# Attention and mixture of experts in one kernel: scores and foldings of a single batch over eight array tiles, and the second batch's exponentials by column on ScalarE

## The chip, the cores and the metric

One core of a Trainium2 chip runs the whole program. The metric is device time in microseconds, the median of several runs; lower is better. TensorE multiplies matrices into PSUM, VectorE, ScalarE and GpSimd work on tiles (GpSimd on SBUF alone), and SyncE issues nearly all DMA transfers.

## The reference

Eight batches, eight heads, 576 positions, head width 64. Each head first packs its keys and values with 32 learned queries `p`, and the positions then attend to the 32 packed rows. The result goes through four experts with a hidden width of 1024, weighted by given probabilities.

```
s = softmax(p k^T / 8);  packed = s v            # 32 rows a head
out = softmax(q packed^T / 8) packed             # 576 rows a head
x = out as (B*S, H*D);  pr = dp / (sum dp + 1e-9)
y = sum over e of pr[:, e] * (relu(x w1[e]) w2[e])
```

All data is fp32. Softmaxes subtract the row's maximum and divide by the sum plus 1e-9.

## The kernel before, in words

The attention's second product is never made for itself: the packed rows are multiplied into `w1` (`g_form`, the *folding*), and the experts' hidden layer comes from the attention weights times the folded matrix. Where fp32 accuracy is wanted from a single pass, an operand is split into a high part (a cast on ScalarE) and a low part (a subtraction); tiles `xh`, `xl` hold the two parts of a batch's attention weights, `ghl` those of a folded matrix, `st` and `tt` those of the second layer's operands. The second layer multiplies blocks by a seven-product scheme (`ORDER`).

**Units.** The main loop goes over 64 units: a batch and a chunk of 512 hidden columns (half of an expert). Batches go in pairs, chunks inside. The first units are batch 0 chunk 0, batch 0 chunk 1, batch 1 chunk 0, batch 1 chunk 1. In each unit there are seven products (`product`, 12 matmuls each), two products ahead their operands are made (`s_operand`: sums on VectorE, cast on ScalarE, subtraction on GpSimd), and in between come four projections of the next unit (`mm1_groups`, 12 matmuls each), foldings for a later chunk, and steps of the attention of later batches.

**Attention of a batch.** The eight heads are two groups of four (`g`). `pack_unit` loads K (L149) and V (L154, L157), makes scores (L122), takes the maximum (L171), exponentiates with the row sum (L177), turns the weights over (L192 to L195), multiplies them into V (L201), scales (L207 or L209) and puts the packed rows into `ppbd` (L105 or L104). `tok_unit` loads the queries (L230), makes scores, turns them by VectorE so that the 32 packed rows of each position lie along the free dimension (L237), takes maxima (L242), subtracts (L251), exponentiates all 576 columns at once (L254), sums (L257), divides (L263), turns back (L268) and splits into `xh` and `xl` (L269, L270 by L104 and L108). With `relief` scores are first copied out of PSUM by ScalarE (L169), the small scalings and additions run on ScalarE, and the exponential is 18 activations of 32 columns, each with its own maximum as bias (L247), in place of subtraction and one activation.

**Array tiles.** In scores and foldings a matmul has 64 rows and 32 columns: a quarter of the columns and half of the rows of the array. `cols(b, hh)` gives the half of a 64-column strip by head parity and batch parity, so that the two batches of a pair never use the same tile. For a pair the matmuls of both batches go out in turn, on eight tiles; for one batch four tiles are used, one group after the other. Each fp32 matmul is two instructions.

**The batches.** Batch 0 goes through an opening stage of some 40 us, with the chain of one group a step behind the other's, a warm-up of 22 matmuls with the identity and the forming of the first second-layer weights. Batch 1 (`second`) has a chain of generators: `wavefront` runs the pack units of its two groups in turn, then the two token units; `SECOND` says how many of its steps are emitted behind each product of units 0 and 1, and what is left is drained in unit 1 behind product 3, ahead of the folding of chunk 0. Later batches come as pairs, one group at a time; the third and fourth with `relief`. Batch 1 borrows tiles: K and queries lie in `xh2`, `xl2`, `xh3`, `xl3`, and V of its second group lies in `xl3`, which the second group's queries take over.

**Order.** Tile framework: the order on each engine comes from a planner that simulates the program and takes ready instructions by their place in the code; each engine runs its queue in order, and so does SyncE's DMA queue. By hand stand in order: `together` (the matmuls of a set stay together, and TensorE's other work keeps its side of it) and a few edges by `after`. PSUM is four double-bank tiles `dbl`.

Of the kernel before, what the change touches and what calls it, by code (L numbers as in the profile page):

```python
# [16 lines left out]
P = 128  # L17
# [22 lines left out]
def attention_moe(ctx: ExitStack, tc: tile.TileContext, q, k, v, p, dp, w1, w2, out):  # L40
# [56 lines left out]
    def cols(b, hh):  # L97

        i = (hh + b) % 2
        return slice(i * NPK, (i + 1) * NPK)  # L100
# [21 lines left out]
    def scores(bs, g, stationary, moving):  # L122

        pss = {b: dbl() for b in bs}
        calls = []
        for c in range(2):
            for j in range(2):
                for hh in range(2):
                    for b in bs:
                        p0 = 2 * j * NPK + cols(b, hh).start  # L130
                        calls.append(dict(
                            out=pss[b][p0:p0 + NPK, c, 0:HS], lhsT=stationary(b, 2 * g + j, hh),
                            rhs=moving[b][hh * D:(hh + 1) * D, j, c * HS:(c + 1) * HS], start=True, stop=True,
                        ))
        together(calls)
        return pss
# [3 lines left out]
    def pack_unit(bs, g, new, relief=False):  # L140
# [3 lines left out]
        for b in bs:  # L144
# [3 lines left out]
            kts[b] = new(b, [P, 2, S], "kt")  # L148
            nc.sync.dma_start(out=kts[b], in_=k[b][:, 2 * g:2 * g + 2, :])  # L149
        yield  # L150

        def load_v(b):
            vt, vr = new(b, [P, nfull, 4 * D], "vt"), new(b, [P, 4 * D], "vr")
# [6 lines left out]
        vt = load_v(bs[0])  # L160
        yield
        pss = scores(bs, g, lambda b, pr, hh: pts[b][hh * D:(hh + 1) * D, pr, :], kts)
        a1s, rss = {}, {}
        for b in bs:
            nb = small.tile([P, 1], F32, name="nb")
            a1s[b] = new(b, [P, S], "a1")
            a1v, raw = a1s[b].rearrange("p (c s) -> p c s", c=2), pss[b][:, :, 0:HS]
# [10 lines left out]
            rss[b] = small.tile([P, 1], F32, name="rs")  # L178
            if relief:
                nc.scalar.activation(out=rss[b], in_=sm, func=AF.Copy, bias=1e-9)  # L180
            else:
                nc.vector.tensor_scalar_add(rss[b], sm, 1e-9)
            nc.vector.reciprocal(out=rss[b], in_=rss[b])
        yield
        prs = slice(2 * g, 2 * g + 2)
        for b in bs:
            if b != bs[0]:
                vt = load_v(b)
            at = new(b, [P, len(SC), P], "at")
            ps = dbl()  # L190
            for c in range(nfull):
                tr(out=ps[:, 0, c * P:(c + 1) * P], in_=a1s[b][:, c * P:(c + 1) * P], identity=ident)  # L192
            tr(out=ps[0:r, 1, 0:P], in_=a1s[b][:, nfull * P:S], identity=ident)
# [4 lines left out]
            for c, (_, n) in enumerate(SC):  # L198
                for h in range(4):
                    p0 = h // 2 * 2 * NPK + cols(b, h % 2).start  # L200
# [13 lines left out]
            for hh in range(2):  # L214
                hi_of(
                    ppbd[b % 4][hh * D:(hh + 1) * D, prs, cols(b, hh)], psv[:, :, cols(b, hh)],
# [7 lines left out]
    def tok_unit(bs, g, new, eng=nc.vector, hi_eng=nc.scalar, lo_eng=nc.gpsimd, relief=False):  # L224
        qts, a2s = {}, {}
        for b in bs:
            if g == 0:
                xs[b] = (xpool.tile([P, NG, S], F32R, name=f"xh{b % 4}"), xpool.tile([P, NG, S], F32R, name=f"xl{b % 4}"))
            qts[b] = new(b, [P, 2, S], "kt")
            nc.sync.dma_start(out=qts[b], in_=q[b][:, 2 * g:2 * g + 2, :])  # L230
        yield
        pss = scores(bs, g, lambda b, pr, hh: ppbd[b % 4][hh * D:(hh + 1) * D, pr, cols(b, hh)], qts)
        for b in bs:
            a2s[b] = new(b, [P, S // 32, NPK], "a1")
            a2f = a2s[b].rearrange("p a n -> p (a n)")
            for c in range(2):
                nc.vector.transpose(out=a2f[:, c * HS:(c + 1) * HS], in_=pss[b][:, c, 0:HS])  # L237
        yield
        for b in bs:
            a2 = a2s[b]  # L240
# [442 lines left out]
```

## Time and profile before

| | us |
|---|---|
| median of 3 runs | 1300.62 (1300.3 to 1301.6) |
| the profiled execution, in all | 1302.57 |
| its span on the core | 1300.7 |
| TensorE busy | 1274.4 (98%) |
| VectorE busy | 954.7 (73%) |
| GpSimd busy | 859.4 (66%) |
| ScalarE busy | 495.7 (38%) |

The span is what the engines' records cover; the profiled execution's own time is longer by what lies before and behind. Busy time of TensorE is modelled from its pipelined matmuls. L67 is the helper of all plain matmuls, L70 of transposes and L75 of those in sets; L104 and L105 are `hi_of`, L108 is `lo_of`. So a row is read by its tiles, not by its line alone. Times in rows are counted from the start of the span.

### The profile page before, as it was taken

To read this page: it belongs to the slowest core of one execution; us is meant where nothing else is said; L and a number is where in the kernel's file an instruction comes from. 1 tells how busy PE (TensorE), PEld (TensorE's weight loads), DVE (VectorE), ACT (ScalarE), POOL (GpSimd) and SP (SyncE) were. 2 spreads that over 40 slices of the span, in tenths; PEclk is the share of its full clock that TensorE was granted. 3 is DMA by queue.
4 is the path that set the end of the run, shared out by engine and by line. 5 is a ranking of instruction groups with operands and counts; after the bars stand their busy time and mean duration, and the time that the engine had idled before them with its cause. 6 is when DMAs were issued, how large, how long until landed. Compare 5 with 4: busy or idle time off the path is not lost.

```text
span 1300.7 us, 26860 instructions
## 1 busy us (share of the span) xinstructions
PE 1274.4 (98%) x10764; PEld 1181.6 (91%) x10764; DVE 954.7 (73%) x1310; ACT 495.7 (38%) x886; POOL 859.4 (66%) x572
## 2 busy tenths in 40 slices
PE   6899999999999999999999999999999999999997
PEld 4789999998999989999999999999999999999997
DVE  6686677899975666987685666789668566666668
ACT  3444535646334333333335333333233433333321
POOL 4778888798995545666578454476558655555556
PEclk8999999999999999999999999999999999999998
DMA  9785646544465543454444456433345533434422
GB/s 350 282 305 204 218 165 226 181 149 167 148 219 194 173 155 124 164 176 155 144 154 164 150 174 194 160 115 115 130 156 203 164 130 123 124 110 153 130 98 73
DMA packets 89979, 218.42 MB, mean 168 GB/s; under 512 B 9088, under 2 KB 31744, under 8 KB 89856
## 3 DMA queue, kind: packets, MB, share of 16 engines
q1 hardware_dynamic: 89184, 216.57, 49.4%
q8 instruction: 86, 1.41, 0.4%
q14 instruction: 37, 0.30, 0.1%
q10 hardware_dynamic: 672, 0.15, 0.1%
HBM read 177.81 MB, written 38.87 MB: 167 GB/s over the span
## 4 chain that ended last, share of the span: by engine, by line
PE 84%; POOL 7%; DVE 5%; issue 2%; DMA 2%; ACT 1%; POOLq 0%; SPq 0%; DVEq 0%; ACTq 0%
PE dbl L67 77%; PE dbl L75 6%; POOL st L108 4%; POOL tt L108 2%; DVE sblk L361 1%; POOL b L398 1%; PE dbl L70 1%; POOL acc L478 1%; DVE ablk L336 1%; DMA xl<-in_q 1%; DVE nb L171 0%; DMA ablk<-in_w 0%; DVE ghl L108 0%; POOL xl L108 0%; DVE a L263 0%
## 5 line engine op out<-in xcount | busy, mean ns | idle before, releaser
L67 PEld LDWEIGHTS dbl<-st,tt 128*128 128x128 f32 x5376 | 730.3, 188 | 61.2 <-POOL st L108 36.2
L67 PE MATMUL dbl<-st,tt 128*128 128x288 f32 x5376 | 774.1, 298 | 5.1 <-POOL st L108 4.7
L108 POOL TENSOR_TENSOR st<-sblk,st 128x576 fp32r<-128x576 f32 x256 | 397.5, 1560 | 208.7 <-ACT st L104 203.5
L67 PE MATMUL dbl<-xh,ghl 128*128 128x288 f32 x2048 | 418.9, 296 | 5.4 <-DVE ghl L108 3.0
L108 POOL TENSOR_TENSOR st<-ablk,st 128x576 fp32r<-128x576 f32 x192 | 288.4, 1505 | 182.7 <-ACT st L104 175.1
L428 DVE TENSOR_TENSOR acc<-dbl,acc 128x576 f32<-128x576 f32 x385 | 289.1, 753 | 118.8 <-PE dbl L67 116.1
L67 PEld LDWEIGHTS dbl<-xh,ghl 128*128 128x128 f32 x2048 | 330.7, 189 | 7.9 <-DVE ghl L108 4.4
L336 DVE SCALAR_TENSOR_TENSOR ablk<-dbl,pbt 128x576 f32<-128x576 f32 x256 | 192.5, 753 | 163.6 <-PE dbl L67 162.3
L67 PE MATMUL dbl<-xl,ghl 128*128 128x288 f32 x1024 | 301.8, 295 | 0.7 <-DVE xl L108 0.7
L104 ACT CAST st<-sblk 128x576 fp32r<-128x576 f32 x256 | 173.0, 676 | 290.0 <-DVE sblk L361 198.4
L104 ACT CAST st<-ablk 128x576 fp32r<-128x576 f32 x192 | 129.7, 676 | 217.3 <-PE dbl L67 206.2
L67 PEld LDWEIGHTS dbl<-xl,ghl 128*128 128x128 f32 x1024 | 193.0, 189 | 0.9 <-DVE xl L108 0.9
L104 ACT CAST ghl<-dbl 128x512 fp32r<-128x512 f32 x128 | 74.8, 586 | 150.6 <-PE dbl L75 92.1
L361 DVE TENSOR_TENSOR sblk<-ablk 128x576 f32<-128x576 f32 x128 | 122.9, 961 | 9.5
L108 DVE TENSOR_TENSOR ghl<-dbl,ghl 128x512 fp32r<-128x512 f32 x128 | 87.4, 685 | 10.4 <-ACT ghl L104 6.7
L75 PE MATMUL dbl<-wraw,ppbd 64*32 64x512 f32 x1024 | 73.7, 600 | 0.2 <-DMA wraw<-in_w 0.2
L361 DVE TENSOR_TENSOR sblk<-ablk,sblk 128x576 f32<-128x576 f32 x64 | 66.3, 1036 | 5.8
L108 POOL TENSOR_TENSOR tt<-b,tt 128x512 fp32r<-128x512 f32 x42 | 62.2, 1491 | 2.1 <-ACT tt L104 2.0
L361 DVE TENSOR_TENSOR sblk<-sblk,ablk 128x576 f32<-128x576 f32 x64 | 57.9, 904 | 1.7
L478 POOL TENSOR_TENSOR acc<-acc,acc 128x576 f32<-128x576 f32 x28 | 47.4, 1702 | 16.2 <-DVE acc L428 16.1
L426 ACT COPY acc<-dbl 128x576 f32<-128x576 f32 x56 | 35.9, 641 | 41.2 <-PE dbl L67 40.6
L478 DVE TENSOR_TENSOR acc<-acc,acc 128x576 f32<-128x576 f32 x21 | 32.2, 1534 | 4.8 <-POOL acc L478 4.6
(90 smaller groups left out, 439.2 us busy)
## 6 DMA issues: line engine op xcount, KB each, us to landing
tt<-td SPq DMA_DIRECT2D x182, 512.0 KB, 4.3
wraw<-in_w SPq DMA_DIRECT2D x136, 256.0 KB, 3.1
td<-tt SPq DMA_DIRECT2D x56, 512.0 KB, 3.5
pbt<-pnd SPq DMA_DIRECT2D x32, 288.0 KB, 4.2
out<-acc SPq DMA_DIRECT2D x32, 288.0 KB, 2.3
kt<-in_k SPq DMA_DIRECT2D x14, 576.0 KB, 5.3
kt<-in_q SPq DMA_DIRECT2D x14, 576.0 KB, 5.4
vt<-in_v SPq DMA_DIRECT2D x15, 512.0 KB, 5.7
```

Source lines behind the costliest of these rows:

```text
L67: on_pe(nc.tensor.matmul(**kw))
L70: on_pe(nc.tensor.transpose(**kw))
L75: ins = nc.tensor.matmul(**kw).ins
L104: return nc.scalar.copy(out=dst, in_=src)
L108: return eng.tensor_tensor(out=dst, in0=src, in1=hi.bitcast(F32), op=ALU.subtract)
L336: nc.vector.scalar_tensor_tensor(out=a, in0=ps[:, :, 0:HS], scalar=0.0, in1=pbt[b][:, c * HS:(c + 1) * HS].rearrange("p (o t) -> p o t", o ...
L361: nc.vector.tensor_tensor(out=t, in0=blk(x), in1=blk(y), op=op)
L398: eng[m].tensor_tensor(out=blk[place], in0=blk[x], in1=blk[y], op=ALU.subtract)
L426: nc.scalar.copy(out=accs[b, i], in_=psv)
L428: nc.vector.tensor_tensor(out=accs[b, i], in0=psv, in1=accs[b, i], op=ALU.add)
L478: eng.tensor_tensor(out=m[dst], in0=m[x], in1=m[y], op=op)
```

## The change

`cols` takes the group too, so that the two groups of one batch use different tiles, as two batches do. `scores`, `pack_unit`, `tok_unit` and `g_form` take a list of items (batch, group) in place of a list of batches and one group.

- *Foldings of one batch* (four calls: opening stage, units 0, 1 and 2) put both groups' matmuls out in turn, eight tiles, into the two halves of one `dbl`. For a pair nothing changes.
- *Batch 1* has one pack unit and one token unit with both groups, in place of two interleaved ones each: K of both, V of both, scores of both side by side, then each group's rest in turn. Both run with `relief`. The chain has 9 + 12 steps instead of 12 + 10; `SECOND` stays.
- With `relief` the division of the token weights stays on the group's engine (VectorE for the first, GpSimd for the second), and the scaling of packed values is now always on VectorE (before, ScalarE with `relief`).
- Batch 0's opening stage keeps one unit for each group, and later pairs keep one group with two batches.

```diff
-    def cols(b, hh):
-        i = (hh + b) % 2
+    def cols(b, hh, g):
+        i = (hh + b + g) % 2
         return slice(i * NPK, (i + 1) * NPK)
...
-    def scores(bs, g, stationary, moving):
-        pss = {b: dbl() for b in bs}
+    def scores(items, stationary, moving):
+        pss = {it: dbl() for it in items}
...
-                    for b in bs:
-                        p0 = 2 * j * NPK + cols(b, hh).start
+                    for b, g in items:
+                        p0 = 2 * j * NPK + cols(b, hh, g).start
...
-        vt = load_v(bs[0])
+        both = items[0][0] == items[-1][0]
+        vts = {it: load_v(*it) for it in (items if both else items[:1])}
         yield
...
-            if relief:
-                nc.scalar.mul(ppn, ps[:, 0, 0:D], rss[b])
-            else:
-                nc.vector.tensor_scalar_mul(ppn, ps[:, 0, 0:D], rss[b])
+            nc.vector.tensor_scalar_mul(ppn, ps[:, 0, 0:D], rss[it])
...
-    def tok_unit(bs, g, new, eng=nc.vector, hi_eng=nc.scalar, lo_eng=nc.gpsimd, relief=False):
+    def tok_unit(items, new, engs=(nc.vector, nc.vector), hi_eng=nc.scalar, lo_eng=nc.gpsimd, relief=False):
...
     def g_form(bs, ch, raws):
-        for g in range(NG):
+        def run(items):
             ps = dbl()
-            pss = {b: ps[:, b % 2] for b in bs}
+            pss = {it: ps[:, i] for i, it in enumerate(items)}
             calls = []
             for hs in range(4):
-                pr, hh = 2 * g + hs // 2, hs % 2
-                rows = slice(hh * D, (hh + 1) * D)
-                for b in bs:
-                    c0 = (hs // 2) * 2 * NPK + cols(b, hh).start
+                for b, g in items:
+                    pr, hh = 2 * g + hs // 2, hs % 2
+                    rows = slice(hh * D, (hh + 1) * D)
+                    c0 = (hs // 2) * 2 * NPK + cols(b, hh, g).start
...
+        if len(bs) == 1:
+            run([(bs[0], g) for g in range(NG)])
+            yield
+        else:
+            for g in range(NG):
+                run([(b, g) for b in bs])
+                yield
...
+    ITEMS = [(1, g) for g in range(NG)]
     second = chain(
-        wavefront([pack_unit([1], g, second_tile(g)) for g in range(NG)], 1),
-        wavefront([tok_unit([1], g, second_tile(2 + g), nc.gpsimd if g else nc.vector) for g in range(NG)], 1),
+        pack_unit(ITEMS, second_tile(("xh2", "xl2")), relief=True),
+        tok_unit(ITEMS, second_tile(("xh3", "xl3")), (nc.vector, nc.gpsimd), relief=True),
     )
     SECOND = {0: (4, 3, 3, 3, 2, 2, 2), 1: (2, 20)}
```

## Rows read from the trace of the kernel before

**Rows 1.** The page, busy time of each engine: us, share of the span and instructions.

```profile
PE 1274.4 (98%) x10764; PEld 1181.6 (91%) x10764; DVE 954.7 (73%) x1310; ACT 495.7 (38%) x886; POOL 859.4 (66%) x572
```

**Rows 2.** The table by stretch: bounds and length in us, busy us and instructions of TensorE, its weight loads, VectorE, ScalarE and GpSimd, then the granted clock, the DMA share and GB/s. Four long stretches, and one of 4 us from a second table.

```profile
0.00:60.00 60.00, 46.44 (x478) 35.36 (x479) 37.55 (x68) 25.39 (x49) 34.60 (x30) 0.91 0.88 316
40.00:60.00 20.00, 17.74 (x213) 13.50 (x212) 12.58 (x21) 12.17 (x24) 15.15 (x11) 1.00 0.67 246
60.00:80.00 20.00, 19.84 (x164) 16.53 (x163) 18.87 (x32) 10.50 (x17) 18.66 (x13) 1.00 0.94 311
...
100.00:300.00 200.00, 197.84 (x1778) 182.85 (x1777) 154.29 (x199) 98.94 (x211) 172.16 (x116) 1.00 0.54 187
...
84.00:88.00 4.00, 4.00 (x32) 4.00 (x31) 1.57 (x3) 0.00 (x0) 1.12 (x1) 1.00 1.01 391
```

**Rows 3.** Waits of TensorE from 40 to 100 us, the two longest: what waited and for whom, us in total, times, longest.

```profile
PE dbl L70 <- ACT a L177: 1.0, 1, 1.0
PE dbl L67 <- ACT at L194: 0.8, 1, 0.8
```

**Rows 4.** Timeline of TensorE around the foldings (the matmuls from wraw and ppbd): start us, us, engine, line, operation, out<-in, shapes, count. Three of one batch, and one of a pair at 139.76; the row behind one shows what starts next.

```profile
41.34 1.92 PE L75 MATMUL dbl<-wraw,ppbd 64*32 64x512 f32 x16
...
77.05 1.92 PE L75 MATMUL dbl<-wraw,ppbd 64*32 64x512 f32 x16
78.91 1.86 PE L67 MATMUL dbl<-st,tt 128*128 128x288 f32 x12
...
90.25 1.92 PE L75 MATMUL dbl<-wraw,ppbd 64*32 64x512 f32 x16
...
139.76 1.09 PE L75 MATMUL dbl<-wraw,ppbd 64*32 64x512 f32 x16
140.78 1.86 PE L67 MATMUL dbl<-st,tt 128*128 128x288 f32 x12
```

**Rows 5.** Timeline of TensorE in the opening stage: the second half of the first folding, the first projection and the first product; the idle time before a row and what ended it stand at its end.

```profile
19.50 1.57 PE L75 MATMUL dbl<-wraw,ppbd 64*32 64x512 f32 x8 [0.19 <-DMA wraw<-in_w]
...
28.04 0.53 PE L67 MATMUL dbl<-xh,ghl 128*128 128x288 f32 x2 [1.86 <-ACT xh L104]
...
39.55 1.86 PE L67 MATMUL dbl<-st,tt 128*128 128x288 f32 x12 [1.17 <-POOL st L108]
```

**Rows 6.** Timeline of TensorE at the scores: of the second batch's pack unit (xh and xl hold its K), of its token unit (xh and xl hold its queries) with the product behind the first group's, and of a pair's pack unit with the product behind it.

```profile
47.58 1.18 PE L75 MATMUL dbl<-xh,pt 64*32 64x288 f32 x16
48.57 1.15 PE L75 MATMUL dbl<-xl,pt 64*32 64x288 f32 x16
...
63.06 1.17 PE L75 MATMUL dbl<-xh,ppbd 64*32 64x288 f32 x16
64.17 1.85 PE L67 MATMUL dbl<-st,tt 128*128 128x288 f32 x12
66.18 1.17 PE L75 MATMUL dbl<-xl,ppbd 64*32 64x288 f32 x16 [0.16 <-DMA xl<-in_q]
...
144.17 1.20 PE L75 MATMUL dbl<-kt,pt 64*32 64x288 f32 x32
145.30 1.87 PE L67 MATMUL dbl<-st,tt 128*128 128x288 f32 x12
```

**Rows 7.** Groups of instructions by line with each shape apart, whole run: line, engine, operation, out<-in, shapes, count, then busy us and mean ns of one, then idle time before. Exponentials by column (L247) and whole (L254), the subtraction on GpSimd, the copy of a pack's scores, the small copies of packed values on ScalarE, turns and maxima on VectorE.

```profile
L247 ACT ACTIVATE a<-a,m 128x32 f32<-128x32 f32 x72 | 16.3, 310 | 0.0
...
L237 DVE STREAM_TRANSPOSE a<-dbl 128x288 f32<-128x288 f32 x32 | 12.8, 453 | 3.3 <-PE dbl L75 3.3
...
L242 DVE TENSOR_REDUCE m<-a 128x18 f32<-128x576 f32 x16 | 11.7, 732 | 0.1
...
L254 ACT ACTIVATE a<-a 128x576 f32<-128x576 f32 x12 | 8.2, 686 | 15.7 <-DVE a L251 14.2 <-POOL a L251 1.4
...
L169 ACT COPY a<-dbl 128x576 f32<-128x576 f32 x4 | 2.4, 643 | 3.2 <-PE dbl L75 3.2
...
L104 ACT COPY ppbd<-dbl 64x64 f32<-64x64 f32 x8 | 1.6, 202 | 0.0
...
L251 POOL TENSOR_TENSOR a<-a,m 128x576 f32<-128x576 f32 x1 | 1.2, 1161 | 0.0
```

**Rows 8.** Timeline of ScalarE in a token unit of the third and fourth batch, in which the exponentials run by column: the first scaling of maxima, the first item's exponentials, and the second item's cast of turned weights.

```profile
245.57 0.22 ACT L245 ACTIVATE m<-m 128x18 f32<-128x18 f32 x1
...
246.36 3.93 ACT L247 ACTIVATE a<-a,m 128x32 f32<-128x32 f32 x18
...
268.40 0.68 ACT L104 CAST xh<-at 128x576 fp32r<-128x576 f32 x1 [1.81 <-DVE at L268]
```

**Rows 9.** Timelines around the second batch's token unit: SyncE's issue of the second group's queries, GpSimd's subtraction for the second group's low part, and TensorE's first projections from the batch's high parts (80.61) and from the second group's low part (86.99).

```profile
58.01 0.33 SPq L230 DMA_DIRECT2D xl<-in_q  x1
...
83.69 1.43 POOL L108 TENSOR_TENSOR xl<-at,xh 128x576 fp32r<-128x576 f32 x1 [1.60 <-ACT xh L104]
...
80.61 0.42 PE L67 MATMUL dbl<-xh,ghl 128*128 128x288 f32 x2
...
86.99 0.30 PE L67 MATMUL dbl<-xl,ghl 128*128 128x288 f32 x1
```

**Rows 10.** The table by stretch for TensorE alone: bounds, length, busy us and instructions, granted clock, DMA share, GB/s.

```profile
26.00:28.00 2.00, 0.17 (x2) 1.00 1.11 384
...
29.00:35.00 6.00, 5.75 (x24) 0.50 1.03 387
```

More of the change, by code (lines that the diff above doesn't have):

```diff
@@ L138, in attention_moe, with pack_unit @@
     pts = {}
-    def pack_unit(bs, g, new, relief=False):
+    def pack_unit(items, new, relief=False):
         nfull = S // P
@@ L177, in pack_unit @@
             nc.scalar.activation(out=a1v, in_=raw, func=AF.Exp, scale=SCALE, bias=nb, accum_out=sm)
-            rss[b] = small.tile([P, 1], F32, name="rs")
+            rss[it] = small.tile([P, 1], F32, name="rs")
             if relief:
-                nc.scalar.activation(out=rss[b], in_=sm, func=AF.Copy, bias=1e-9)
+                nc.scalar.activation(out=rss[it], in_=sm, func=AF.Copy, bias=1e-9)
             else:
-                nc.vector.tensor_scalar_add(rss[b], sm, 1e-9)
-            nc.vector.reciprocal(out=rss[b], in_=rss[b])
+                nc.vector.tensor_scalar_add(rss[it], sm, 1e-9)
+            nc.vector.reciprocal(out=rss[it], in_=rss[it])
         yield
[L185 to L189, printed above, removed]
+        for b, g in items:
+            it = b, g
+            if it not in vts:
+                vts[it] = load_v(*it)
+            vt = vts[it]
+            prs = slice(2 * g, 2 * g + 2)
+            at = new(b, g, [P, len(SC), P], "at")
             ps = dbl()
             for c in range(nfull):
-                tr(out=ps[:, 0, c * P:(c + 1) * P], in_=a1s[b][:, c * P:(c + 1) * P], identity=ident)
-            tr(out=ps[0:r, 1, 0:P], in_=a1s[b][:, nfull * P:S], identity=ident)
+                tr(out=ps[:, 0, c * P:(c + 1) * P], in_=a1s[it][:, c * P:(c + 1) * P], identity=ident)
+            tr(out=ps[0:r, 1, 0:P], in_=a1s[it][:, nfull * P:S], identity=ident)
             nc.scalar.copy(out=at[:, 0:nfull, :], in_=ps[:, 0].rearrange("p (c s) -> p c s", s=P))
@@ L199, in pack_unit @@
                 for h in range(4):
-                    p0 = h // 2 * 2 * NPK + cols(b, h % 2).start
+                    p0 = h // 2 * 2 * NPK + cols(b, h % 2, g).start
                     mm(
@@ L266, in tok_unit @@
             yield
-            a2t = new(b, [P, S], "at")
+            a2t = new(b, g, [P, S], "at")
             marks[b, g, "turn"] = nc.vector.transpose(out=a2t, in_=a2.rearrange("p a n -> p (a n)")).ins
@@ L502, in drain, with att_tile @@
             pass
-    def att_tile(b, shape, name):
+    def att_tile(b, g, shape, name):
         return att.tile(shape, F32, name=name, bufs=2 if name in ("kt", "a1") else 1)
@@ L563, in attention_moe, with second_tile, new @@
     AT_FIRST = ((4, pack_unit, 0), (7, pack_unit, 1), (9, tok_unit, 0), (12, tok_unit, 1))
-    def second_tile(n):
-        def new(b, shape, name):
-            if name == "kt" or name == "vt" and n == 1:
-                return xpool.tile(shape, F32, name=("xh2", "xl2", "xh3", "xl3")[n] if name == "kt" else "xl3")
-            return att_tile(b, shape, "kt" if name == "vr" else name)
+    def second_tile(names):
+        def new(b, g, shape, name):
+            if name == "kt" or name == "vt" and g == 1:
+                return xpool.tile(shape, F32, name=names[g] if name == "kt" else "xl3")
+            return att_tile(b, g, shape, "kt" if name == "vr" else name)
         return new
+    ITEMS = [(1, g) for g in range(NG)]
     second = chain(
-        wavefront([pack_unit([1], g, second_tile(g)) for g in range(NG)], 1),
-        wavefront([tok_unit([1], g, second_tile(2 + g), nc.gpsimd if g else nc.vector) for g in range(NG)], 1),
+        pack_unit(ITEMS, second_tile(("xh2", "xl2")), relief=True),
+        tok_unit(ITEMS, second_tile(("xh3", "xl3")), (nc.vector, nc.gpsimd), relief=True),
     )
@@ L590, in attention_moe @@
                     drain(back)
-                    back = make(pair, g, att_tile, relief=sb == 0)
+                    back = make([(n, g) for n in pair], att_tile, relief=sb == 0)
         gsteps = nothing
```

64 lines of the change are left out of this document (32 added, 32 removed).

## The prediction, made before the changed kernel ran

> **What bounds the kernel now.** I began with the page's busy shares: TensorE is busy 1274.4 of 1300.7 us, the other engines 38% to 73% [rows 1]. Next the table by stretch, to see where TensorE isn't full: it lacks 13.6 us in the first 60 us, 2.3 us of these in 40 to 60, then 0.2 us in 60 to 80 and 2.2 us in the 200 us after 100 [rows 2]. The reader is to see that from 60 us on the kernel is one long TensorE queue: a microsecond of matrix work taken out there is a microsecond off the end, if the operands still come in time. The same table names the neighbours: in 60 to 80 us VectorE has 18.87 and GpSimd 18.66 of 20 us, ScalarE 10.50. Third, TensorE's own waits in 40 to 100 us, where nearly all of the change lies: 1.0 us for an exponential (L177) and 0.8 us for the copy of turned scores (L194), most of the 2.3 us that are missing there [rows 3]. Last, TensorE's timeline for the price of each changed group, and the other engines' for the second batch's chain.
>
> The sum goes against the profiled execution's own time, 1302.57 us (span 1300.7 plus 1.87 around it). The median of the runs is 1300.62, that is 1.95 less; I carry the difference over to it.
>
> **The change part by part.**
>
> *Foldings of one batch.* Now both groups go one after the other, four array tiles each: 16 instructions from 77.05 until the next product starts at 78.91, 1.86 us. A pair's folding of one group has 16 instructions of the same shape in eight tiles: 139.76 to 140.78, 1.02 us [rows 4]. The changed folding of one batch has just this form, so each saves 0.84 us. Four calls: the one at 41.34 (unit 0), 77.05 (unit 1) and 90.25 (unit 2) lie in a full TensorE queue: 3 x 0.84 = 2.52 us. The fourth, in the opening stage, I cost at 0: its later matmuls wait for weights from DMA (its second half starts at 19.50), and what follows on the path, the first projection at 28.04, waits for ScalarE's cast of the turned weights, not for the folding [rows 5]. Side by side, the first half also waits for the weights of the second, inside that cover. If the cover were gone it could be worth -0.84 to +0.84 us; I leave it at 0.
>
> *Scores of the second batch.* Pack: 47.58 for the first group, 48.57 for the second, the last ends at 49.72 (48.57 + 1.15): 2.14 us. Tokens: 63.06 to 64.17, 1.11 us, and the second group's at 66.18, of the same length: 2.22 together. A pair's scores, 32 instructions, run 144.17 to 145.30, 1.13 us [rows 6]. Saved: 1.01 + 1.09 = 2.10 us. With the foldings 4.62 us of TensorE's queue go.
>
> *ScalarE's new work.* The exponentials of the tokens: 36 of 128x32 instead of two of 0.69 us. The 72 of the later batches took 16.3 us, 0.226 us each, so 36 cost 8.15 us, net +6.8 us [rows 7]. Score copies 2 x 0.64 = 1.3 us; the four small copies of packed values 4 x 0.20 = 0.8 us; some eight tiny scalings and additions, by the length of those copies about 1.6 us. Together near +10 us on ScalarE between about 43 and 80 us, where it has 22.7 of 40 us now: 33 of 40. It isn't full, but queued behind a run of six to eighteen exponentials (1.3 to 3.9 us) stand the casts of the products' operands, for which GpSimd and then TensorE wait. Two products of lookahead (1.7 us each, 78.91 to 80.61 [rows 4, 9]) with projections between them cover that. In the later relief stretch 18 exponentials ran as one block of 3.93 us [rows 8] without a wait of TensorE's there. I cost this delay at 0; without the cover one block would cost at most its 3.93 us.
>
> *What leaves VectorE and GpSimd.* One subtraction of 1.16 us on GpSimd, one on VectorE, the four small copies [rows 7] and the tiny ones: about 3 us of VectorE where it is the fullest. As TensorE isn't waiting for it, I count 0 for itself; it shortens the chain below. Scaling of the packed values in the next two batches goes back to VectorE: four small operations, hidden, 0 (bounds: -1.0 us, the longest of TensorE's waits in rows 3, and +0.8 us, four of the small copies).
>
> *The pack chain, moved.* It has 4 + 3 + 3 steps in unit 0 as before, but the scores come in product 0's share instead of product 1's, up to 43.2 - 0.84 = 42.4 instead of 47.6. Each group's chain gains the copy (0.64 us) ahead of the maximum. Projections and products that stood before the scores now can stand between scores and transposes. The two waits of 1.0 and 0.8 us there may go, or grow by the two copies: bounds -1.8 to +1.3 us; I take 0. On SP the second batch's V loads and the token loads move up together; the second group's queries go into the tile in which its V lay, so they wait for the pack's last use of it: issued at 58.01, they let the scores start at 66.18 with a wait of 0.16 us [rows 6, 9]. Now both groups' token scores wait for that load; nothing on TensorE but they depends on it, and products are at hand to go first.
>
> *The token chain.* Before: scores of the first group at 63.06, second group's low part done at 83.69 + 1.43 = 85.12, used by TensorE at 86.99 (the first use of either part of this batch is at 80.61) [rows 6, 9]. That use moves up by what is saved ahead of it, 0.84 + 1.01 + 1.09 + 0.84 = 3.8 us, to 83.2. The new chain starts when the second group's queries are there, now for both groups: 66.2 less the 3 to 6 us by which the pack moves up, 60 to 63. By the old latency of the second group, 85.12 - 66.18 = 18.9 us, it ends at 79 to 82, in time. By the later relief stretch it takes 2.4 us (four turns of 0.45, one maximum of 0.73, less one that overlaps with the first scaling), 22.8 us from the first scaling (245.57) to the second item's cast (268.40) [rows 7, 8], and 2.1 us for cast and subtraction, 27 us in all: it ends at 87 to 90, 4 to 7 us late. In that stretch nobody waited for it and ScalarE also cast formed weights; and after 80 us, where ScalarE and VectorE now mostly wait (84 to 88 us: 0 and 1.57 of 4 us [rows 2]), there is room for the chain's end. TensorE can also put remaining products first, as it did. I lie nearer to the old latency: 61.5 + 18.9 + half of the exponentials' net 6.8 us is 83.8, some 0.6 us late; I take 1.0 us of wait, with 0 and 7 as ends.
>
> *The Trainium skill on this.* After the token scores TensorE's next instruction is a product (64.17), while VectorE takes 0.9 us per group to empty the banks: nothing waits for that [rows 6, 7]. The Trainium skill, "TensorEngine Tiling (Array Packing)", section Performance Considerations (PSUM Bottleneck), says that tiling makes TensorE faster but not the emptying of PSUM, which can then become the bound. By that rule the scores' 2.10 us would buy nothing; the case is the third rival below, and the row at 64.17 speaks against it.
>
> Sum: -2.52 - 2.10 + 1.0 = -3.6 us: 1302.57 - 3.6 = 1298.97 in the profiled execution, 1300.62 - 3.6 = 1297.0 as a median.
>
> **Rivals.**
> 1. *The second batch is late by as much as was saved.* The chain takes 23 to 25 us from 61.5 and the wait is 2 to 4 us and more, without other loss: at 4 us -4.62 + 4 = -0.6, 1300.0 (1298.0 to 1303). For it: rows 8's latency, and 36 exponentials in one in-order queue. Against: the earlier start and the emptier engines after 80 us.
> 2. *Slower: the same wait, and the clock falls.* In the opening TensorE was busy 0.17 of 2 us in 26 to 28 us, and the granted clock stood at 0.50 for 29 to 35 us [rows 10]: six to seven us at 1.2 instead of 2.4 GHz, some 3.3 us lost. If the second batch's operands come so late that TensorE stands still for about 5 us near 80 us, the clock goes too: -4.62 + 5 + 3.3 = +3.7, 1304.3. The clock went in the opening after a wait of 1.86 us [rows 5]; with its 3.3 us the result is slower than before from a wait of 1.3 us, and by more than a measurement's doubt from 3.9, that is, where the low part is done at 87.1 or later: scores at 61 and a chain of 26 us. For it: the queries' load that holds both groups. Against: TensorE has two products and half of the projections to put into such a hole, and these would keep its clock up.
> 3. *Narrow tiles buy nothing in the scores* because emptying four half banks takes 1.8 us against 1.13 of matrix work: -2.52 + 1.0 = -1.5, 1299.1. Against it: the pair's scores at 144.17 are followed by a product without a gap [rows 6]. The rule is that of the Trainium skill, "TensorEngine Tiling (Array Packing)", PSUM Bottleneck, cited above.
> 4. *More than the sum:* the waits of 1.8 us go too and none comes: -4.62 - 1.8 = -6.4, 1294.2.
>
> **How the numbers follow.** Forecast, 1295.3 to 1298.5: 0.48. Rival 1: 0.22. Rival 2: 0.14. Rival 3: 0.06. Rival 4: 0.10. A measurement tells 0.2% from nothing, 2.6 us: faster is under 1298.0, slower over 1303.2. Faster: of the forecast 0.43, rival 4 0.10, together 0.53. Slower: rival 2's 0.14 and 0.02 of rival 1: 0.16. Within: 0.31. Range: from 1293.8 (most of rival 4) to 1303.2 (rivals 1 and 3 but for a rest, not rival 2).
>
> **What would show it.** Right: foldings of one batch with 16 instructions to the next in about 1.0 us and scores with 32 in 1.13 at four and two places, TensorE's instruction count the same, and TensorE's waits in 40 to 95 us at 1 to 3 us. The second batch's first projection at about 77, not 80.6 us. Wrong: a TensorE wait for the second batch's high or low part, or for an operand of a product behind a block of exponentials; a granted clock under 1 after 40 us; a wait for the queries' load of over 1 us; the first product starting at another time than 39.55 us [rows 5]. The forecast falls if this chain costs over 2 us, or if the planner's order later in the kernel shifts by as much.

## The result, and the profile after

The changed kernel takes 1311.94 us (median of 6 runs, 1309.66 to 1313.32) against 1300.67 us for the kernel before in the same sitting: ratio 1.0081, 95% interval 1.0071 to 1.0091. It is slower, by 0.8%; the forecast was 1297.0 us, and the range ended at 1303.2. The profiled execution took 1311.35 us, its span 1309.3 us. One run of an experiment below, *token exponential whole*, was disturbed (1375.87 us): it is left out of that kernel's median, and as it is the traced one, no trace of that kernel is read.

The busy times on the page of the changed kernel, beside [rows 1]:

```profile
PE 1273.8 (97%) x10764; PEld 1181.9 (90%) x10764; DVE 950.7 (73%) x1303; ACT 505.0 (39%) x930; POOL 856.1 (65%) x571
```

TensorE's count is the same and its busy time hardly is less, though matrix work was saved. ScalarE gained 9.3 us. What was saved came back as matmuls at a lower clock, as the rows below show, and the longer span is idle time: 35.5 us of TensorE's span instead of 26.3. Where it lies, TensorE's timeline of the changed kernel shows (start us, us, operation, count; idle time before a row at its end). The line numbers have moved: L178 is the exponential of the pack unit (L177 before), L247 the exponentials by column.

```profile
39.50 1.86 PE L67 MATMUL dbl<-st,tt 128*128 128x288 f32 x12 [0.54 <-POOL st L108]
41.29 1.09 PE L75 MATMUL dbl<-wraw,ppbd 64*32 64x512 f32 x16
42.17 0.40 PE L75 MATMUL dbl<-xl,pt 64*32 64x288 f32 x1
...
48.62 1.33 PE L70 MATMUL dbl<-ident,a 128*128 128x128 f32 x5 [5.28 <-ACT a L178]
49.61 3.23 PE L67 MATMUL dbl<-st,tt 128*128 128x288 f32 x12
...
62.98 0.67 PE L75 MATMUL dbl<-xh,ppbd 64*32 64x288 f32 x2
64.08 0.40 PE L75 MATMUL dbl<-xl,ppbd 64*32 64x288 f32 x1 [0.44 <-DMA xl<-in_q]
...
65.21 1.85 PE L67 MATMUL dbl<-st,tt 128*128 128x288 f32 x12
...
79.72 4.98 PE L67 MATMUL dbl<-st,tt 128*128 128x288 f32 x24 [3.08 <-POOL st L108]
84.63 1.09 PE L75 MATMUL dbl<-wraw,ppbd 64*32 64x512 f32 x16
85.65 1.85 PE L67 MATMUL dbl<-st,tt 128*128 128x288 f32 x12
...
99.46 3.45 PE L67 MATMUL dbl<-st,tt 128*128 128x288 f32 x24
...
118.28 1.95 PE L75 MATMUL dbl<-wraw,ppbd 64*32 64x512 f32 x32
```

Three rows of the kernel before to hold against these: the product behind the turns, the first products of unit 2, and the first folding for a pair.

```profile
51.26 1.82 PE L67 MATMUL dbl<-st,tt 128*128 128x288 f32 x12
...
92.11 3.60 PE L67 MATMUL dbl<-st,tt 128*128 128x288 f32 x24
...
109.97 1.95 PE L75 MATMUL dbl<-wraw,ppbd 64*32 64x512 f32 x32
```

The first product starts where it did (39.50; 39.55 in [rows 5]). The folding with 32 instructions, the first for a pair, starts at 118.28; in the kernel before it starts at 109.97. This stretch, from the first product to that folding, is 78.78 us long against 70.42: 8.36 of the 8.6 us of span. I call it *the stretch* and use it for the experiments too, since it begins behind the opening stage.

TensorE's waits in the changed kernel, 40 to 100 us (us in total, times, longest), against the two of [rows 3]:

```profile
PE dbl L70 <- ACT a L178: 5.3, 1, 5.3
PE dbl L67 <- POOL st L108: 3.1, 1, 3.1
PE dbl L67 <- POOL xl L108: 0.9, 1, 0.9
PE dbl L70 <- DVE ppn L209: 0.8, 2, 0.4
```

The tables by stretch, with all engines first (to be held against [rows 2]) and then TensorE alone with its granted clock:

```profile
40.00:60.00 20.00, 13.91 (x190) 11.69 (x189) 10.32 (x16) 13.48 (x31) 12.11 (x9) 0.83 0.69 257
60.00:80.00 20.00, 16.48 (x141) 14.98 (x141) 13.81 (x20) 15.06 (x54) 10.00 (x8) 1.00 0.64 238
```

```profile
46.00:48.00 2.00, 0.00 (x0) 0.58 1.01 377
48.00:50.00 2.00, 1.38 (x7) 0.50 0.31 106
...
80.00:82.00 2.00, 2.00 (x12) 0.61 0.13 49
```

In the first long wait, and behind the second, the granted clock fell from 1.00 to about 0.50, that is from 2.4 to 1.2 GHz. The product at 49.61 took 3.23 us, [rows 4] has 1.86 for twelve matmuls; the 24 matmuls at 79.72 took 4.98 us, two such products at full clock, at 68.50 and at 73.28, took 3.36.

The account from the first product of unit 0 to that of unit 2 (99.46; 92.11 in the kernel before), where the kernel lost 59.96 - 52.56 = 7.40 us:

| | us |
|---|---|
| foldings: 3 x 0.84 | -2.52 |
| pack scores: 42.17 to 43.35 instead of 2.14 us | -0.96 |
| token scores: 62.98 to 65.21, 2.23 us with the wait for the queries inside; before 2.22 and a wait of 0.16 | -0.15 |
| waits: 5.28 + 3.08 + 0.94 + 2 x 0.41, before 1.02 + 0.76 + 0.33 | +8.01 |
| clock: 3.23 - 1.82, 4.98 - 3.36, turns 0.99 - 0.52 | +3.50 |
| sum | +7.88 |

The sum is 0.48 us more than was lost; which small rows hold that is not traced.

**Where the first wait comes from.** ScalarE in the changed kernel, 43 to 50 us:

```profile
45.46 0.59 ACT L104 CAST ghl<-dbl 128x512 fp32r<-128x512 f32 x1 [0.76 <-DVE ghl L108]
45.95 1.19 ACT L170 COPY a<-dbl 128x576 f32<-128x576 f32 x2
...
47.70 0.78 ACT L178 ACTIVATE a<-a,nb 128x576 f32<-128x576 f32 x1
```

Scores end at 43.35. ScalarE copies them out only at 45.95, behind its casts for the products and the folding, of which the last is shown; then come maximum, scaling and exponential, and only then the turns at 48.62. In the kernel before, product 1 and a projection stood ahead of the scores (47.58), not between scores and turns. By then VectorE was through with the folding's low parts and waited for the scores, so that the turns followed after 1.02 us. VectorE's first maximum in the kernel before:

```profile
48.82 0.76 DVE L171 TENSOR_REDUCE nb<-dbl 128x1 f32<-128x576 f32 x1 [0.38 <-PE dbl L75]
```

Now the scores come while ScalarE is still busy with casts, the turns are the very next thing in TensorE's queue, and product 1 stands behind them.

**Where the second comes from.** ScalarE again, 68 to 79 us, and the GpSimd row that follows from it:

```profile
68.59 4.13 ACT L247 ACTIVATE a<-a,m 128x32 f32<-128x32 f32 x19
...
73.15 1.39 ACT L247 ACTIVATE a<-a,m 128x32 f32<-128x32 f32 x6
...
74.95 1.39 ACT L247 ACTIVATE a<-a,m 128x32 f32<-128x32 f32 x6
...
76.34 1.17 ACT L247 ACTIVATE a<-a,m 128x32 f32<-128x32 f32 x5
77.40 1.24 ACT L104 CAST st<-sblk 128x576 fp32r<-128x576 f32 x2
```

```profile
78.15 2.91 POOL L108 TENSOR_TENSOR st<-sblk,st 128x576 fp32r<-128x576 f32 x2 [8.33 <-ACT st L104]
...
90.39 1.44 POOL L108 TENSOR_TENSOR xl<-at,xh 128x576 fp32r<-128x576 f32 x1 [0.21 <-ACT xh L104]
```

36 exponentials (19 + 6 + 6 + 5) run from 68.59 to 77.5; between the blocks stand two copies of results and a small addition, but no cast of a product's operand. GpSimd, which makes the low parts, stands still for 8.33 us; TensorE lives on its lookahead and then waits 3.08 us. The row at 90.39 is the second group's low part, the end of the token chain.

### The profile page after: what moved, and what is told of

Read it like the earlier page. It is cut to its first block, busy times and chain, and to the rows that moved or that the text cites. A ratio compares the mean times of both kernels' runs of the same rounds, so it can differ in the third digit from the quotient of the medians.

```text
span 1309.3 us, 26888 instructions
## 1 busy us (share of the span) xinstructions
PE 1273.8 (97%) x10764; PEld 1181.9 (90%) x10764; DVE 950.7 (73%) x1303; ACT 505.0 (39%) x930; POOL 856.1 (65%) x571
## 4 chain that ended last, share of the span: by engine, by line
PE 83%; DVE 7%; POOL 6%; ACT 2%; issue 1%; DMA 1%; DVEq 0%; SPq 0%; ACTq 0%; POOLq 0%
PE dbl L67 77%; PE dbl L75 5%; POOL st L108 3%; DVE sblk L368 2%; POOL tt L108 1%; DVE ablk L343 1%; PE dbl L70 1%; DVE acc L450 1%; ACT a L247 1%; DVE a L263 0%; DVE ghl L108 0%; POOL xl L108 0%; DVE acc L435 0%; DVE nb L172 0%; POOL acc L485 0%
```

## Experiments: the two long waits

Theory: the loss comes from these two places, and the eight tiles are innocent. Rivals: VectorE's load, the scalings moved to it, or the tiles themselves. Medians, ratios to the kernel before in the same sitting (1300.7 to 1301.4 us), and the stretch in the profiled execution:

| kernel | median us | ratio, 95% interval | stretch us |
|---|---|---|---|
| before | 1300.67 | | 70.42 |
| the change | 1311.94 | 1.0081 [1.0071, 1.0091] | 78.78 |
| turns behind product 1 | 1310.35 | 1.0067 [1.0052, 1.0082] | 77.24 |
| token exponential whole | 1309.81 | 1.0053 [1.0032, 1.0074] | |
| both of these | 1304.92 | 1.0028 [1.0019, 1.0038] | 73.35 |
| steps spread over three units | 1305.37 | 1.0035 [1.0024, 1.0047] | 74.06 |
| no `relief` for batch 1 | 1308.12 | 1.0050 [1.0035, 1.0065] | 75.66 |
| scalings on ScalarE | 1311.17 | 1.0073 [1.0058, 1.0088] | 78.53 |
| TensorE kept busy in the hole | 1311.83 | 1.0078 [1.0061, 1.0094] | 84.03 |
| foldings alone | 1302.16 | 1.0008 [0.9998, 1.0018] | 70.14 |
| scores and late foldings, steps in turn | 1302.67 | 1.0012 [1.0003, 1.0021] | 71.92 |
| foldings, batch 0's by group | 1302.56 | 1.0002 [0.9993, 1.0011] | 72.14 |
| scores and all foldings, steps in turn | 1302.72 | 1.0010 [1.0001, 1.0018] | 72.72 |
| before, turns later | 1301.81 | 1.0015 [1.0006, 1.0024] | 71.25 |
| foldings by group, turns later | 1305.16 | 1.0027 [1.0018, 1.0037] | 70.82 |
| in turn, turns later | 1304.62 | 1.0029 [1.0018, 1.0040] | 72.59 |

Each stretch is that of one execution. In eight of these traces the first product starts at 37.3 to 38.1 us, in the other seven, the kernel before and the change among them, at 39.5 to 40.3. In the kernel before the granted clock stood at 0.50 from 29 to 35 us [rows 10]; in *foldings alone*, whose first product starts at 37.71, it was 1.00 on the mean of the opening. In four of the early ones unit 0's folding then waits 0.30 to 0.91 us for weights from DMA, in none of the late ones. So an early start can come back in part as a longer stretch, and a microsecond of difference between an early and a late trace says nothing.

**Turns behind product 1.** Of the chain's steps, product 0 issues three instead of four, so the first group's turns come behind product 1.

```diff
-    SECOND = {0: (4, 3, 3, 3, 2, 2, 2), 1: (2, 20)}
+    SECOND = {0: (3, 4, 3, 3, 2, 2, 2), 1: (2, 20)}
```

> The changed kernel with SECOND[0] starting 3, 4 in place of 4, 3: the first group's turns are emitted behind product 1 instead of behind product 0, nothing else. Theory: TensorE's wait of 5.3 us at 48.6 us and the half clock from 49 to 53 us go, the wait at 79.7 us stays: 7 us off the changed kernel, about 1304.5. Rival (the chain is what takes the time, wherever its turns are queued; it ends later and the wait near 80 us grows by as much): 1309 to 1312.

TensorE's timeline of this kernel:

```profile
47.72 0.77 PE L70 MATMUL dbl<-ident,a 128*128 128x128 f32 x5 [0.90 <-ACT a L178]
...
60.38 0.40 PE L75 MATMUL dbl<-xl,ppbd 64*32 64x288 f32 x1 [1.66 <-DMA xl<-in_q]
...
76.03 4.81 PE L67 MATMUL dbl<-st,tt 128*128 128x288 f32 x24 [3.08 <-POOL st L108]
```

The time is the rival's. The first wait is gone, 0.90 instead of 5.28 us, but the stretch is only 1.54 us shorter: the token scores now wait 1.66 us for queries, three waits of 0.5 to 0.75 us stand in the rest of the pack chain, and the second long wait stays whole.

**Token exponential whole.** `relief` off in the token unit alone.

> The changed kernel with relief off in the second batch's token unit alone (one exponential of 576 columns, subtraction on VectorE or GpSimd); pack unit as changed. Theory (36 exponentials ahead of the products' casts make the wait at 79.7 us): that wait, its clock loss and the 0.9 us at 88.8 go, 5 to 6 us off the changed kernel, near 1306. Rival (VectorE, relieved by it, becomes what is waited for, as in the run without relief, where a folding's low part came 2.1 us late): 1308 to 1310.

The three runs took 1304.93, 1309.81 and 1310.02 us, so this gain is known only roughly, some 2 us; the median is the rival's.

**Both of these.**

```diff
-        tok_unit(ITEMS, second_tile(("xh3", "xl3")), (nc.vector, nc.gpsimd), relief=True),
+        tok_unit(ITEMS, second_tile(("xh3", "xl3")), (nc.vector, nc.gpsimd)),
...
-    SECOND = {0: (4, 3, 3, 3, 2, 2, 2), 1: (2, 20)}
+    SECOND = {0: (3, 4, 3, 3, 2, 2, 2), 1: (2, 20)}
```

> Both repairs: turns behind product 1 (SECOND[0] = 3, 4, 3, ...), and the token unit without relief; pack unit with relief, scores and foldings in eight tiles. Theory (two separate waits): both gone, 1304 to 1306, that is 4 to 6 us off the run with the turns later alone, still above the kernel before by the waits for the queries and for packed values. Rival (VectorE late): 1308 or more.

Alone they gave 1.6 and some 2 us, both together 7.0: while one long wait stands, most of what the other gives back is waited out further on. Theory's 1304 to 1306 us for both together came true. **Spread** is the other way to take both waits away: the turns behind product 1, and the token unit with `relief` as in the change, but its steps dealt out so that a few exponentials at a time lie between the casts.

```diff
-    SECOND = {0: (4, 3, 3, 3, 2, 2, 2), 1: (2, 20)}
+    SECOND = {0: (3, 4, 3, 1, 1, 1, 1), 1: (2, 2, 2, 20)}
```

> The changed kernel with SECOND = {0: (3, 4, 3, 1, 1, 1, 1), 1: (2, 2, 2, 20)}: the turns behind product 1 as in the run before, and the token unit's steps spread over two more products, so that two casts of products' operands stand ahead of most of the second group's exponentials on ScalarE. Theory: beside the first wait the second one (3.1 us, and about 1.5 us of clock) goes too, 4 us off the run with the turns later alone, near 1306. Rival (the second batch is then late at its own projections by as much): 1309 to 1312.

It gains 6.6 us with all 36 exponentials by column, 5.0 us more than the turns behind product 1 alone, and no wait of TensorE in the stretch is longer than 1.0 us. So the second wait came from their lying in one block, not from their cost.

**The rivals.** Without `relief` in both units, and with the next batches' small scalings back on ScalarE:

> The changed kernel with relief off in both units of the second batch: no score copies, one exponential for 576 columns, small steps on VectorE. Theory (two waits: turns queued ahead of product 1, and products behind 36 exponentials): the wait at 79.7 us (3.1), the one at 88.8 (0.9) and the clock's loss behind them (about 1.7) go, the wait at 48.6 us shrinks from 5.3 to about 4 and its clock loss of about 2 us stays: near 1304.5 us. Rival one (ScalarE's new work is the whole cause): below 1299. Rival two (one unit for both groups is the whole cause): 1310 or more.

> The changed kernel with the packed values of the third and fourth batch scaled on ScalarE again, nothing else. Theory: the wait of TensorE for L209 between 240 and 300 us (1.5 us) goes, about 1310.4. Rival (that wait is only another one's shadow): 1311.9, the same.

Without `relief` the first wait is still 4.13 us: the copies of scores were a small part of it, and now the maxima wait on VectorE (45.35) behind the low parts of the folding. The 1308.12 us lie between the theory's 1304.5 and rival two's 1310: a wait of 2.08 us for a folding's low part, which VectorE makes, is new at 84.45. The scalings' place takes TensorE's wait for them from 1.5 to 0.4 us and moves its busy time between 240 and 300 us from 58.24 to 59.33 (59.75 in the kernel before, whose work lies some 8 us earlier), but the time only within its interval: not shown to cost anything in the end.

**The clock alone.** 22 matmuls with the identity fill the hole behind the pack scores; their result isn't used.

> The changed kernel with 22 matmuls of the identity with itself (as in the warm-up) between the second batch's pack scores and its turns, into the hole of 5.3 us; nothing waits for them. Theory (the hole also costs the clock): granted clock 1.00 from 44 to 54 us, product 1 in 1.8 instead of 3.2 us, about 2 us off, 1310. Rival (what the clock lost there is waited for later anyway): 1311.9, the same.

Product 1 took 1.83 us at a granted clock of 1.00, but the time is that of the change, as the rival said. TensorE's timeline further on, in an execution that was the slowest of the four (1317.11 us; the others 1310.58 to 1313.01):

```profile
64.66 0.66 PE L76 MATMUL dbl<-xl,ppbd 64*32 64x288 f32 x1 [2.65 <-DMA xl<-in_q]
66.76 3.25 PE L68 MATMUL dbl<-st,tt 128*128 128x288 f32 x12
```

What the clock gave back, the scores waited out for the queries in this execution, and the clock fell there instead (0.50 from 64 to 70 us).

## Experiments: what the saved matrix work is worth

The kernel without either long wait was still 3.7 us slower than before; in its trace the token scores wait 2.00 us for queries, the packed values 1.2 us for VectorE, and unit 0's folding 0.91 us for weights. So the savings themselves were tried.

**Foldings alone** (all four; batch 1's chain as before).

> Only the foldings of a single batch go over eight tiles (columns by group too); the second batch keeps its interleaved units, narrow scores and whole exponentials, and packed values of the third and fourth batch are scaled on ScalarE as before. Theory (the loss sits in the second batch's chain, the foldings save what their rows say): 3 x 0.84 us off the kernel before, about 1298.1 us against its 1300.7. Rival (eight tiles give nothing back in a single batch, or the loss comes with the new columns): 1300.7 or more.

TensorE's timeline of this kernel at unit 0's folding and the turns:

```profile
39.49 1.04 PE L75 MATMUL dbl<-wraw,ppbd 64*32 64x512 f32 x2
40.83 1.74 PE L75 MATMUL dbl<-wraw,ppbd 64*32 64x512 f32 x14 [0.30 <-DMA wraw<-in_w]
42.50 1.87 PE L67 MATMUL dbl<-st,tt 128*128 128x288 f32 x12
...
49.39 0.77 PE L70 MATMUL dbl<-ident,a 128*128 128x128 f32 x5 [1.94 <-ACT a L178]
```

With the groups' matmuls alternating the folding needs all four weight tiles at its start. Here it starts 1.8 us sooner than in the kernel before, the tiles are not there, and it took 3.01 us instead of 1.86. In the trace of the change, with a late first product, the same folding found its weights there (41.29 to 42.17). The next three leave the alternating out, or test it:

```diff
-        if len(bs) == 1:
+        if bs == [1]:
             run([(bs[0], g) for g in range(NG)])
```

In the first and the second, batch 0's foldings go group by group. Their tiles still differ by the group, so the second group's matmuls run beside the first's: at unit 0 the trace has 16 instructions in 1.09 us, the row of an eight-tile folding. The narrow folding of the expectations was therefore never run; what these kernels change at unit 0 is that the second half's weights are needed later. *In turn* also means that the wide scores are kept, `relief` is off for batch 1, and the two groups' steps alternate as in the kernel before, with `SECOND[0] = (2, 2, 3, 3, 0, 2, 2)`.

> Second batch's scores of both groups on eight tiles, and wide foldings in units 1 and 2 only; the rest as before: the two groups' steps interleaved stage by stage, scores behind product 1, the exponential as one activation, no copies of scores, batch 0's foldings with four tiles. My theory: the change lost by the place of the turns in TensorE's queue and by the block of exponentials ahead of the casts, not by the eight tiles. Then both long waits (5.3 and 3.1 us) are gone, the clock stays at 1.00 from 40 to 100 us, and the matrix work saved counts: 2.1 us of scores and 1.7 us of foldings, less up to 1 us because both groups' scores wait for the second group's queries: 1297.5 to 1298.5. Rival: what is saved comes back as small waits for GpSimd, VectorE and the queries' load, since these engines are nearly full from 60 to 80 us: 1300 to 1302, ratio 0.999 to 1.001. A third, that eight tiles of one batch in themselves do harm, would give 1303 or more.

> Only the second batch's foldings (units 1 and 2) on eight tiles, all else as before. My theory: the kernel with all foldings wide gained nothing because unit 0's folding waits for four weight tiles at once and pushes the pack chain back; without it the two others are worth what they save, 2 x 0.84 us = 1.7: 1299.5. Rival: the products behind them wait for GpSimd's operands as much longer as the folding is shorter: 1301.2, the time before.

> As the kernel in turn, but with the foldings of the opening and of unit 0 on eight tiles as well. My theory: unit 0's folding loses by waiting for four weight tiles what it saves in matrix work: the same as the kernel in turn, or up to 1 us more. Rival: it gives its 0.84 us: about 1 us less than the kernel in turn.

None of these four gains as a median; the theories of a gain, 1298.1 us, 1297.5 to 1298.5 and 1299.5, failed. In the foldings by group much of that is the clock: its four runs at a mean granted clock of 0.998 or 0.999 took 1299.82 to 1300.35 us, its seven at 0.994 and 0.995 took 1301.65 to 1304.21; the five of the kernel before at 0.998 in that sitting took 1300.31 to 1301.33. So where the clock held, the medians of these few runs differ by 0.3 of the 2.5 us: the eight tiles do no harm in the foldings, and little good. The traced execution is the slowest, 1304.21 us. TensorE's timeline of it shows both, the saving that is waited out and the fall of the clock:

```profile
41.41 1.09 PE L75 MATMUL dbl<-wraw,ppbd 64*32 64x512 f32 x16
...
50.83 0.95 PE L70 MATMUL dbl<-ident,a 128*128 128x128 f32 x5 [1.94 <-ACT a L178]
51.43 3.23 PE L67 MATMUL dbl<-st,tt 128*128 128x288 f32 x12
...
80.56 1.83 PE L67 MATMUL dbl<-st,tt 128*128 128x288 f32 x12 [0.98 <-DVE s L264]
...
95.63 1.86 PE L67 MATMUL dbl<-st,tt 128*128 128x288 f32 x12 [0.69 <-POOL st L108]
```

VectorE behind that folding, first in the kernel before, then in this one:

```profile
43.43 1.80 DVE L361 TENSOR_TENSOR sblk<-ablk,sblk 128x576 f32<-128x576 f32 x1
45.18 1.29 DVE L108 TENSOR_TENSOR ghl<-dbl,ghl 128x512 fp32r<-128x512 f32 x2
```

```profile
43.52 1.81 DVE L371 TENSOR_TENSOR sblk<-ablk,sblk 128x576 f32<-128x576 f32 x1
45.27 1.29 DVE L108 TENSOR_TENSOR ghl<-dbl,ghl 128x512 fp32r<-128x512 f32 x2
```

Both executions start the first product within 0.1 us of each other (39.55 and 39.63). TensorE finishes the folding some 0.8 us sooner, VectorE takes it up at the same time as before, 45.2, since it is busy with sums for the products. The turns stand at 50.83 against 50.74 [rows 3 has their wait, 1.0 us; here 1.94]. At unit 0 nothing is saved, and behind the longer wait the clock fell to 0.50 in this execution: 3.23 us for the product behind the turns, product 2. Behind the other two foldings 0.98 and 0.69 us are waited out for operands, against 0.84 us that each saves.

**Is it the turns or the feeders?** The last three put one more product between scores and turns, in the kernel before and in two variants. Counted from 0, as in the rest of this text, it is product 2; the expectations call it product 1.

```diff
-    SECOND = {0: (4, 3, 3, 3, 2, 2, 2), 1: (2, 20)}
+    SECOND = {0: (4, 2, 3, 4, 2, 2, 2), 1: (2, 20)}
```

> The kernel before with one move: product 1 ahead of the turns of the second batch's pack unit, the second group's packed values behind product 2. It takes out a wait of 1.0 us for the exponential and one of 0.8 us for the copy of turned scores, and no matrix work. If TensorE's queue is the bound: 1301.3 less 1.0 to 1.8 us, 1299.5 to 1300.3. If VectorE, ScalarE and GpSimd set the pace, product 1's early end is waited out further on: 1301.3, as before.

> All three foldings of a single batch behind the opening on eight tiles (batch 0's by taking its two groups one behind the other on different tiles), and the same move of the turns. Theory A (the wait for the turns and the clock ate the gain): the time of the kernel before with the move less 2.5 us, 1297 to 1298. Theory B (the feeding engines set the pace; in the run without the move VectorE's sums and ScalarE's casts kept their times to 0.1 us while the folding was 0.8 us shorter): the same as the kernel before with the move, within 0.5 us, and waits for operands of 0.3 to 1.0 us behind each folding.

> The kernel in turn (scores of both groups on eight tiles, the second batch's foldings too) with product 1 ahead of both groups' turns. Theory A: the wait of 2.6 us and the fall of the clock behind it go, and 2.1 us of scores and 2.5 of foldings count: 1296.5 to 1298. Theory B: the wait and the clock's part go (about 2 us less than the run without the move, 1302.7), the rest is waited out for operands: 1300 to 1301.3.

TensorE's timeline of the kernel before with that move:

```profile
52.59 0.65 PE L67 MATMUL dbl<-vt,at 128*32 128x64 f32 x32 [1.34 <-ACT at L194]
...
59.19 0.27 PE L70 MATMUL dbl<-ident,ppn 128*64 128x128 f32 x1 [1.05 <-DVE ppn L209]
```

The waits of 1.0 and 0.8 us are gone, and 1.34 and 1.05 us have come in their place; the median is no better than that of the kernel before (ratio 1.0015). Unit 0's folding in the second of the three kernels, and the second group's turns in the third:

```profile
39.52 2.40 PE L75 MATMUL dbl<-wraw,ppbd 64*32 64x512 f32 x16
```

```profile
54.26 0.77 PE L70 MATMUL dbl<-ident,a 128*128 128x128 f32 x5 [2.10 <-ACT a L178]
...
55.91 3.19 PE L67 MATMUL dbl<-st,tt 128*128 128x288 f32 x12
```

With the foldings the stretch is 70.82 against 71.25 us, both at a full clock and both with an early first product (37.73 and 38.11). At unit 0 nothing was saved: the folding took 2.33 us, where a weight load waited 0.41 us for DMA, and 2.13 us with the move alone. Of the 1.68 us of the other two foldings 0.43 are left in the stretch. So theory A falls, and the trace is as theory B said for the foldings. As medians the two variants are slower than theory B said, 1305.16 and 1304.62 us. In the first, the mean granted clock sorts the runs: 1300.95 and 1300.98 us at 0.997 and 0.998, 1303.80 to 1307.71 us in the nine at 0.991 to 0.996; the traced one is of the two. In which stretch those nine lost the clock, and why so many of them, no trace shows: that stays open. In the second the long wait only moved: the second group's turns wait 2.10 us, and the product behind them takes 3.19 us at a granted clock of 0.50. No traced kernel has both groups' scores on eight tiles without a wait of 2 us or a fall of the clock in the stretch, so what their 2.1 us are worth by themselves is not shown.

## Why the prediction was wrong

**What held.** The size of the matrix work: foldings with 16 instructions take 1.02 us, pack scores 1.18 us. The first product did not move, though other traces have it anywhere from 37.3 to 40.3 us, so that says little. The token chain's wait came out as forecast, 0.94 us for the low part `xl`, taken as 1.0, but by luck: the second group's low part was done at 91.83 us (90.39 + 1.44) and not at 83.8, some 27.8 us behind the queries (64.08). That is the length of the later relief stretch, 27 us, which the prediction set aside for some 22. That TensorE waited so little goes with the other waits having held it back by then: it came to the first low part at 88.84 us, not near 83.

**Step "The pack chain, moved".** It took 0 with bounds of -1.8 to +1.3 us; it cost 5.28 + 0.82 - 1.78 = +4.3 us of waits, and 1.9 us of clock. I wrote that projections and products "now can stand between scores and transposes". They could not: the chain has fewer and other steps (nine of the pack unit, not the "4 + 3 + 3 steps in unit 0 as before"), and the fourth step of product 0's share, formerly the second group's V load, is now the first group's turns. Counting the steps between the `yield`s would have told it. Moving the turns behind product 1 takes this wait away (0.90 us).

**Step "ScalarE's new work".** Costed at 0, at most the 3.93 us of one block of 18. Both groups' exponentials lay in one run of 36, with no cast among them, and the wait of 3.08 us and 1.6 us of clock followed. The sum of busy time, which I checked ("33 of 40"), was if anything too high: 28.5 us from 40 to 80. The order inside was what mattered.

**Step "Scores of the second batch", tokens.** 1.09 us were to be saved; none was. The two first instructions ran, and the rest waited for the second group's queries, since both groups now start together. I had seen that wait and put nothing on it, because "products are at hand to go first". But a set that stands first in an in-order queue lets nothing go first.

**"A microsecond of matrix work taken out there is a microsecond off the end."** This first step carried the sum, with the condition that operands come in time. They don't: the foldings alone gave a ratio of 1.0008 [0.9998, 1.0018], where -2.5 us would be 0.998. At unit 0 the rows show why: VectorE took the shorter folding up no sooner. That the other feeders pace TensorE in the same way is read from the waits of 0.69 and 0.98 us behind the other foldings, not tested by making a feeder faster.

**Rivals.** Rival 2 had the mechanism: a wait of about 5 us, a fall of the clock, slower. It named the wrong operand and one place near 80 us; there were two places, near 48 and near 77 us, and 1304.3 was too little. Rival 3's rule, "TensorEngine Tiling (Array Packing)", Performance Considerations (PSUM Bottleneck) in the Trainium skill, says that emptying PSUM can become the bound. The trace agrees in part: of the 5.28 us behind the pack scores, the copies out of PSUM took 1.19 for both groups, but they began 2.6 us after the scores had ended, behind casts. Without the copies the wait was still 4.13 us, so what stood ahead in the queue of the emptying engine was the larger part.

## What to carry to other kernels

When steps of a generator are dealt out by count, write down which instruction each count now issues, and what then stands behind it in each in-order queue. Before a saving on a full engine is counted, look at whether its feeders have idle time just there: a busy share of 99% can be a pace set by others. Here a folding that was 0.8 us shorter changed nothing at unit 0. And of two stalls in a row, removing one may show little; try both together before a cause is dropped.

## What the runs showed of the hardware

The clock can fall after a short wait: in the foldings by group it went to 0.50 behind one of 1.94 us, while in the foldings alone the same wait, 1.94 us, left it at 1.00 and the product behind it at 1.82 us. So one profile doesn't settle what a wait costs. And eight tiles needed no alternating in the program: 16 instructions of two groups, one group behind the other, took 1.09 us at unit 0 in the foldings by group, as long as alternating ones in the change, with the tiles of the groups apart in both.
